# A fused attention and PReLU kernel on one core: the states of seven batches in one load, fills of 512 different columns written first, and a new order of all steps

## The chip, the core and the metric

The kernel runs on one core of one Trainium2 chip. TensorE (PE) multiplies matrices, VectorE (DVE), ScalarE (ACT) and GpSimd (POOL) work on elements, SyncE (SP) issues DMAs; DMAs are issued by ACT and POOL as well. Each engine takes its own instructions strictly in the order in which the program lists them, and waits on semaphores where it needs another engine's result. The metric is the device time of one execution in microseconds (us). Before the change it is 210.93 us, the median of 3 runs (210.7 to 211.01).

## The reference

```python
def _attn_ref(x, state):                      # x (8, 8, 512, 64), state (8, 8, 32, 64)
    scores = scale * np.matmul(x, state.transpose(0, 1, 3, 2))
    a = softmax(scores);  xread = np.matmul(a, state)          # tokens read the states
    scores2 = scale * np.matmul(state, x.transpose(0, 1, 3, 2))
    a2 = softmax(scores2); sread = np.matmul(a2, x)            # states read the tokens
    return np.concatenate([xread, sread], axis=2)

def _moe_ref(x, w_in, w_out, alpha):          # x (8 * 544, 512), d_ff = 2048
    h = x @ w_in
    g = np.maximum(h, 0.0) + alpha * np.minimum(h, 0.0)
    return g @ w_out
```

`softmax` stands here for the maximum, exponential, sum and division over the last axis that the reference writes out. Eight batches of 512 token rows and 32 state rows, 8 heads side by side in the 512 columns, go through attention and then through a two-layer network with a PReLU between.

## The kernel before

All work is cut into small steps, and one long string, ORDER (lines 18 to 96), lists them by name in the order in which they are written into the program. Nothing else sets the order of the work: an engine's queue is the list of those steps that fall to it. A step's letters `a`, `v` and `p` say that it goes to ACT, DVE or POOL. The last numbers of some steps name one of six single banks of PSUM (0 to 5) that the step's tile takes; the remaining two banks form one tile, tag `two`, that the scores `sc` of a batch and some of the `m` steps take in turn. A step that takes a bank waits until the readers of the bank's last tile have finished.

The steps that matter here, with b the batch:

- `stc`, `stt`, `sto`, `sbd`: cast, transposition on PE, copy out and pairing of the states that come early (lines 252 to 271). `lst` loads the other states on POOL's queue (line 194), `str` and `sro` transpose them and copy them out in two halves (lines 280 to 289). `lx`, `wi`, `wo` load x of a batch, a quarter of w_in, a quarter of w_out, all on POOL's queue (lines 156, 200, 206).
- Batch 0 has a path of its own: `cx` casts x, `xt` transposes it on PE, `xo` copies it out, `tsc` makes the scores, `smax`, `ssh`, `sexp`, `ssum`, `snorm` the softmax over the states, `at` and `ao` turn the result. `xt` and `xo` also serve batch 1.
- Other batches: `sc` makes the scores (line 314), `sb` turns them in blocks of 32 by 32 (DVE, line 352), `tm`, `nb`, `te` are the maximum, shift and exponential over the tokens (DVE, ACT, ACT, lines 430 to 455), `smax`, `ssh`, `sexp`, `ssum`, `snorm`, `wb` the softmax over the states. `sb`, `tm` and both `te` of a batch read the same tile `sc`. `tt` and `xd` are transpositions by DMA, `rd`, `rdo`, `rt`, `rto` the reads of the states.
- `m.b.f` multiplies the states of a batch with quarter f of w_in (PE, line 535) and `mo` copies the result out as `m`. `F.b.jc` is the first layer: the softmax weights times `m` (PE, 2 matmuls of 512 columns; batch 8 stands for all the state rows). `N` is the negative part (ACT, line 624), `G` the prelu (DVE, line 629).
- The second layer is `S` and `O` for batch 0, and for the others seven half-size products in place of eight: `W` and `U` make sums of the weights and of g, `P` multiplies (PE, 4 matmuls of 256 columns), `K` keeps a partial result, `Q` adds and sends it out.
- `Z` is a fill: a matmul on made-up numbers whose result nobody reads (line 229). Six of them stand ahead of ORDER (line 239).

Of the kernel before, what the change touches and what calls it, by code (L numbers as in the profile page):

```python
# [42 lines left out]
N.2.6 G.2.4 P.1.7.1.1.1 U.1.3.0.p G.2.6 ssh.p.3 P.1.7.0.1 sexp.3 ssum.3.0 P.1.7.1.0 tsum.3 P.1.5.0.0 K.1.4.a P.1.7.0.0
m.3.0.3.4 m.4.3 mo.3.0.a.1 mo.3.0.a.0 rd.3.2 U.1.4.1.p P.1.3.1.1 P.1.3.0.1 P.1.3.1.0 P.1.3.0.0 snorm.v.3 P.2.1.0.0.4
rdo.3.1.a mo.4.3.a P.2.1.1.0 rdo.3.0.a m.4.0.3.0 Q.1.0.1.a m.7.1.2.5 sc.4 mo.7.1.a.0 Q.1.1.1 U.2.1.1.p U.2.2.1.p
P.1.4.0.1 wb.3 P.1.4.1.0 F.3.10.2 mo.4.0.a.0 mo.4.0.a.1 F.3.3.3 sb.4 U.2.1.0.p F.3.1.0 P.2.1.1.1 N.3.10 tm.4 N.3.3
G.3.3 P.1.4.1.1 N.3.1 G.3.1 P.1.4.0.0 Q.1.1.0 P.2.1.0.1 nb.4.a te.4.1 F.3.12.3 G.3.10 F.3.15.0 mo.7.1.a.1 N.3.12
te.4.0 tt.4 F.3.8.1 G.3.12 smax.4 K.2.1.a F.3.2.5 F.3.9.2 N.3.9 N.3.2 sc.0 tm.0 P.2.2.1.1.3 N.3.15 G.3.9 G.3.15
P.2.2.0.1 P.2.6.1.1 P.2.6.0.1 P.2.2.0.0 N.3.8 G.3.8 U.2.2.0.p G.3.2 nb.0.a te.0.1 U.2.3.1.p P.2.6.0.0 P.2.6.1.0 te.0.0
tt.0 P.2.2.1.0 Q.2.0.0 K.2.2.a F.3.11.2 N.3.11 G.3.11 tsum.0 lx.5 xd.5 tsum.4 F.3.7.0 N.3.7 G.3.7 F.3.5.1 N.3.5 G.3.5  # L50
F.3.13.5 N.3.13 U.2.4.1.p G.3.13 ssh.p.4 F.3.6.3 P.2.5.0.0 P.2.5.1.0 P.2.7.1.1.2 N.3.6 F.3.14.0 G.3.6 sexp.4 U.2.3.0.p
N.3.14 G.3.14 F.3.4.1 P.2.7.1.0 P.2.5.0.1 P.2.7.0.1 N.3.4 U.2.4.0.p P.2.5.1.1 K.2.4.a ssum.4.5 rd.0.3 rdo.0.0.a
rdo.0.1.a rd.4.0 lx.6 G.3.4 P.2.7.0.0 Q.2.1.1 P.2.3.1.0 rt.0.3 rto.0.a snorm.v.4 rdo.4.1.a rdo.4.0.a xd.6 lx.7
U.3.1.1.p F.3.0.1 N.3.0 G.3.0 P.2.3.0.1 U.3.1.0.p P.2.4.0.1 P.2.3.1.1 P.2.3.0.0 Q.2.0.1.a m.4.1.3.0 mo.4.1.a.1
m.4.2.5.1 mo.4.2.a.1 sc.5 P.3.1.0.1.4 wb.4 mo.4.1.a.0 tm.5 mo.4.2.a.0 P.3.1.0.0 sb.5 F.4.2.0 N.4.2 G.4.2 F.4.1.1 N.4.1
xd.7 P.2.4.1.0 nb.5.a P.2.4.1.1 U.3.2.1.p P.2.4.0.0 Q.2.1.0 F.4.12.3 G.4.1 F.4.15.5 N.4.12 smax.5 N.4.15 G.4.15
F.4.3.0 N.4.3 F.4.10.2 N.4.10 P.3.2.1.0.1 G.4.3 P.3.2.0.0 te.5.0 G.4.12 P.3.2.1.1 P.3.1.1.0 te.5.1 P.3.1.1.1 P.3.2.0.1
G.4.10 K.3.1.a F.4.6.5 N.4.6 Q.3.0.0 F.4.9.0 F.4.4.3 F.4.13.2 N.4.9 G.4.6 G.4.9 N.4.4 G.4.4 U.3.2.0.p F.4.0.1
P.3.6.1.1 U.3.4.1.p P.3.6.1.0 N.4.13 G.4.13 P.3.6.0.0 N.4.0 G.4.0 P.3.6.0.1 K.3.2.a m.5.0.5.0 sc.6 mo.5.0.a.1
mo.5.0.a.0 tm.6 F.4.11.3 N.4.11 U.3.4.0.p F.4.7.2 N.4.7 sb.6 G.4.7 tt.5 F.4.8.1 F.4.14.0 N.4.14 N.4.8 nb.6.a G.4.8  # L60
te.6.0 G.4.11 smax.6 F.4.5.5 N.4.5 P.3.5.1.0 G.4.14 P.3.5.0.1 U.3.3.1.p P.3.5.0.0 U.3.3.0.p P.3.7.0.0.2 P.3.7.0.1
P.3.5.1.1 ssh.p.5 K.3.4.a P.3.7.1.0 te.6.1 P.3.7.1.1 P.3.3.1.1 sexp.5 G.4.5 rd.5.1 U.4.1.0.p U.4.2.0.p tsum.5
rdo.5.0.a sc.7 rdo.5.1.a m.5.3.3.0 mo.5.3.a.0 Q.3.1.1 ssum.5.5 tt.6 ssh.p.6 tm.7 P.3.3.0.0 mo.5.3.a.1 P.3.3.0.1
P.3.3.1.0 P.3.4.1.1 Q.3.0.1.a U.4.1.1.p U.4.2.1.p P.3.4.0.1 snorm.v.5 U.4.4.0.p m.6.1.1.3 mo.6.1.a.1 m.7.2.0.4
mo.7.2.a.1 P.3.4.0.0 P.3.4.1.0 Q.3.1.0 P.4.1.0.0.3 mo.7.2.a.0 P.4.1.0.1 P.4.1.1.0 P.4.2.1.0.4 wb.5 P.4.2.0.0 P.4.1.1.1
mo.6.1.a.0 U.4.3.1.p nb.7.a sexp.6 ssum.6.0 te.7.0 te.7.1 K.4.1.a sb.7 P.4.2.1.1 P.4.2.0.1 F.5.15.5 N.5.15 Q.4.0.0
F.5.7.1 N.5.7 F.5.13.2 N.5.13 P.4.6.1.1 P.4.6.0.0 G.5.13 G.5.15 G.5.7 P.4.6.1.0 P.4.6.0.1 F.5.6.4 F.5.9.2 F.5.1.5
snorm.v.6 K.4.2.a P.4.5.1.0 P.4.5.0.1 N.5.9 N.5.6 P.4.5.0.0 G.5.6 P.4.5.1.1 N.5.1 G.5.1 G.5.9 F.5.4.1 F.5.10.0 tsum.7
K.4.4.a N.5.4 F.5.12.4 N.5.12 U.4.4.1.p F.5.3.5 P.4.3.0.1 N.5.3 P.4.3.1.1 P.4.3.1.0 G.5.4 rd.6.2 G.5.12 G.5.3 tt.7
rd.7.1 tsum.6 m.7.3.4.5 m.6.0 N.5.10 G.5.10 rdo.6.0.a rdo.7.0.a mo.7.3.v.0 rdo.7.1.a rdo.6.1.a mo.7.3.a.1 rt.1.1  # L70
m.7.0.2.0 m.6.2.5.4 rto.1.v mo.7.0.a.1 P.4.3.0.0 F.5.8.1 mo.6.2.a.0 smax.7 Q.4.0.1.a U.4.3.0.p F.5.0.0 mo.6.2.a.1
F.5.2.5 wb.6 F.8.7.3 P.4.7.1.1.4 P.4.7.0.0 N.5.8 N.5.2 P.4.7.1.0 G.5.8 F.5.11.1 mo.7.0.a.0 N.8.7 G.5.2 G.8.7 F.8.4.2
F.8.8.5 N.5.0 G.5.0 N.5.11 N.8.4 F.5.5.3 G.5.11 N.8.8 G.8.8 N.5.5 G.8.4 F.8.6.0 N.8.6 F.5.14.1 ssh.p.7 F.6.4.5
P.5.2.1.0.2 N.5.14 G.5.5 U.5.1.0.p U.5.2.0.p P.4.7.0.1 P.5.1.1.1.3 G.5.14 P.5.2.1.1 U.5.1.1.p P.5.2.0.0 P.5.1.0.0
G.8.6 N.6.4 Q.4.1.1 P.4.4.1.0 G.6.4 P.4.4.1.1 P.4.4.0.0 sexp.7 P.4.4.0.1 P.5.1.1.0 ssum.7.1 snorm.v.7 P.5.1.0.1
Q.4.1.0 K.5.1.a P.5.2.0.1 Q.5.0.0 F.8.2.0 N.8.2 G.8.2 wb.7 F.6.6.5 N.6.6 G.6.6 F.6.13.1 N.6.13 F.6.11.4 F.6.15.2
N.6.15 G.6.15 N.6.11 G.6.11 F.8.15.0 N.8.15 P.5.6.1.0 U.5.2.1.p P.5.6.0.1 P.5.6.0.0 P.5.6.1.1 K.5.2.a F.7.4.5 G.6.13
# [739 lines left out]
```

## Time and profile before

| what | value |
|---|---|
| median of 3 runs | 210.93 us |
| the profiled execution | 211.77 us |
| its span, first to last instruction | 209.9 us |
| mean granted clock | 1.000 |
| PE, DVE, ACT, POOL busy | 95%, 87%, 70%, 75% |
| HBM read, written | 18.36 MB, 8.91 MB |

Rows of the timeline have the start in us, the duration, the engine, the line, the operation, the tiles (out<-in), the number of instructions merged, and in brackets the engine's idle time before them and what ended it. PEld is PE's loading of weights. Rows of the stages have the stretch, its length, then the busy time of PE, PEld, DVE, ACT and POOL with the number of instructions, the granted clock, the share of the DMA engines and GB/s. Rows of the chain have the start, the time spent, and the engine, tile and line it was spent on. A matmul's duration in a row includes its passage through the array, so that a run of matmuls is counted by the distance from start to start.

### The profile page before, as it was taken

What the parts mean: (1) busy time and instruction counts of PE and PEld (TensorE: products, weight loads), DVE (VectorE), ACT (ScalarE), POOL (GpSimd) and SP (SyncE); (2) the same over time, 40 slices, a digit from 0 to 9 for tenths busy, and PEclk for the clock granted to TensorE, in tenths of its full rate; (3) what the DMA queues carried; (4) which work ended last, traced back from release to release, by engine and by line L of the source; (5) the groups of instructions that cost most, each with busy time, mean ns of one, the idle gap of its engine ahead of it and who ended that gap; (6) DMA issues with size and microseconds to landing.
All of it is one profiled execution on the core that took longest, in us unless ns stands there. A gap on an engine that the chain in (4) does not pass through costs nothing.

```text
span 209.9 us, 5050 instructions
## 1 busy us (share of the span) xinstructions
PE 200.3 (95%) x2000; PEld 133.2 (63%) x2000; DVE 181.8 (87%) x269; ACT 146.6 (70%) x299; POOL 157.9 (75%) x96
## 2 busy tenths in 40 slices
...
GB/s 163 233 204 176 194 199 181 104 118 140 168 172 249 80 100 74 156 178 119 196 282 60 98 107 100 3 52 55 100 0 50 53 50 50 3 0 62 141 125 126
DMA packets 46215, 24.77 MB, mean 118 GB/s; under 512 B 24560, under 2 KB 45680, under 8 KB 46192
## 3 DMA queue, kind: packets, MB, share of 16 engines
...
q10 hardware_dynamic: 544, 0.13, 0.3%
...
HBM read 18.36 MB, written 8.91 MB: 130 GB/s over the span
## 4 chain that ended last, share of the span: by engine, by line
PE 78%; DVE 10%; ACT 7%; DMA 2%; issue 1%; ACTq 0%; DVEq 0%
PE px L732 24%; PE h L574 22%; PE pv L732 13%; PE py L732 6%; DVE g L630 5%; PE o L644 4%; PE h L583 3%; PE m_ps L525 2%; DMA x<-in_x_dram 2%; ACT neg L627 2%; ACT m L549 1%; PE sc L322 1%; ACT osb L661 1%; ACT e L449 1%; ACT XS L488 1%
## 5 line engine op out<-in xcount | busy, mean ns | idle before, releaser
L630 DVE SCALAR_TENSOR_TENSOR g<-neg,oma_sb,h 128x512 f16<-128x512 f32 (+1 forms) x144 | 94.8, 711 | 5.0 <-ACT neg L627 4.0
L627 ACT ACTIVATE neg<-h 128x512 f32<-128x512 f32 (+1 forms) x144 | 75.4, 594 | 12.6 <-PE h L574 10.1
L574 PE MATMUL h<-aT,m 128*128 128x512 f16 x256 | 64.2, 379 | 0.6 <-ACT osb L661 0.3
L732 PEld LDWEIGHTS <-gsum 128*128 128x128 f16 x480 | 46.6, 98 | 9.7 <-issue 0.7
L574 PEld LDWEIGHTS <-m 128*128 128x128 f16 x256 | 24.3, 98 | 24.7 <-issue 2.9
L732 PEld LDWEIGHTS <-g 128*128 128x128 f16 x360 | 34.8, 98 | 7.5 <-issue 1.7
L711 POOL TENSOR_TENSOR gsum<-gsum,g 128x1024 f16<-128x1024 f16 (+1 forms) x14 | 28.8, 2058 | 8.5 <-DVE gsum L711 7.7
L711 POOL TENSOR_TENSOR gsum<-g,gsum 128x1024 f16<-128x1024 f16 (+1 forms) x15 | 29.9, 1997 | 5.1 <-DVE gsum L711 3.2
L732 PE MATMUL px<-ws,gsum 128*128 128x256 f16 x240 | 31.1, 273 | 0.0
L711 POOL TENSOR_TENSOR gsum<-g 128x1024 f16<-128x1024 f16 (+1 forms) x14 | 28.7, 2057 | 3.1 <-DVE gsum L711 3.1
L711 POOL TENSOR_TENSOR gsum<-g,g 128x1024 f16<-128x1024 f16 (+1 forms) x12 | 24.5, 2049 | 6.9 <-DVE g L630 4.3
L748 ACT COPY kept<-px 128x512 f32<-128x512 f32 (+1 forms) x21 | 12.2, 580 | 23.1 <-PE px L732 22.9
L551 ACT CAST m<-m_ps 128x512 f16<-128x512 f32 x36 | 20.0, 626 | 1.5 <-PE m_ps L525 1.5
L392 POOL TENSOR_TENSOR ts<-ts,mx 128x1024 f32<-128x1024 f32 x7 | 13.4, 1913 | 6.7 <-ACT oq L763 4.1
L765 DVE TENSOR_TENSOR oq<-pv,kept 128x512 f32<-128x512 f32 (+1 forms) x16 | 10.4, 651 | 7.9 <-issue 4.4
L732 PE MATMUL py<-w_out_sb,g 128*128 128x256 f16 x120 | 16.6, 273 | 0.2 <-ACT osb L661 0.2
L644 PE MATMUL o<-w_out_sb,g 128*128 128x512 f16 x64 | 16.5, 380 | 0.0
L732 PE MATMUL pv<-ws,gsum 128*128 128x256 f16 x120 | 16.2, 273 | 0.0
L732 PE MATMUL px<-w_out_sb,g 128*128 128x256 f16 x120 | 16.1, 273 | 0.0
L732 PE MATMUL px<-w_out_sb,gsum 128*128 128x256 f16 x120 | 15.9, 273 | 0.0
L732 PE MATMUL pv<-ws,g 128*128 128x256 f16 x120 | 15.2, 273 | 0.0
L525 PE MATMUL m_ps<-w_in_sb,stT 64*32 64x512 f16 x256 | 12.3, 390 | 1.4 <-ACT e L449 1.1
...
## 6 DMA issues: line engine op xcount, KB each, us to landing
...
xg<-in_x_dram POOLq DMA_DIRECT2D x8, 512.0 KB, 6.9
w_in_sb<-in_moe_w_in_dram POOLq DMA_DIRECT2D x4, 512.0 KB, 9.0
w_out_sb<-in_moe_w_out_dram POOLq DMA_DIRECT2D x4, 512.0 KB, 10.7
x<-in_x_dram SPq DMA_DIRECT2D x2, 512.0 KB, 5.5
...
st<-in_state_dram POOLq DMA_DIRECT2D x1, 192.0 KB, 7.6
```

What stands on the lines that cost most here:

```text
L392: engine(e).tensor_tensor(blocks(cols(live["ts", b], j, S)), blocks(scored(b, j)), over_blocks(cols(live["mx", b], j, S // N)), ALU.subtract,)
L525: nc.tensor.matmul(t[N * k : N * (k + 1), :], st_head(b, h)[64 * r : 64 * r + 64, :], w_in_sb[64 * r : 64 * r + 64, c, 512 * f : 512 * (f ...
L551: copier(e)(m_tile(b, f)[:, g, :], t[g])
L574: nc.tensor.matmul(h.rearrange("p (r j s) -> p r j s", r=2, j=2), ms[b, f][:, g, 128 * j : 128 * (j + 1)], weights(b, g), start=(g == 0), ...
L583: nc.tensor.matmul(h, w_in_sb[:, c, 128 * jc : 128 * (jc + 1)], XS[:, c].rearrange("p q n b -> p (q n b)"), start=(c == 0), stop=(c == n_c ...
L627: nc.scalar.activation(neg, h, RELU, bias=0.0, scale=-1.0)
L630: nc.vector.scalar_tensor_tensor(g_tile(b, jc), negs.pop((b, jc)), oma_sb[:, jc : jc + 1], hs.pop((b, jc)), ALU.mult, ALU.add,)
L644: nc.tensor.matmul(outs[b, q], g_tile(b, jc)[:, 128 * q : 128 * (q + 1)], w_out_sb[:, jc, :], start=not begun and jc == 2 * jc2, stop=left ...
L711: engine(e).tensor_tensor(t, x(), y(), op)
L732: nc.tensor.matmul(pbanks[b, name][:, i, :], of(b, c)[:, j, 128 * i : 128 * (i + 1)], moving[:, 4 * c + j, :], start=not begun and j == 0, ...
L748: copier(e)(t, pbanks[b, "x"])
L765: nc.vector.tensor_tensor(osb, pbanks[b, name], kept[b, add], ALU.add)
```

## The change

Only batch 0's states are loaded ahead on ACT's queue; those of the seven other batches come in one load of 14 rows a partition on POOL's queue (192 KB written before, 224 KB now). Batch 1's own cast, transposition and copy go, and each half of `str` and `sro` has 7 groups of 128 columns in place of 6. The fills' operand is one tile of 512 different columns in place of 256 columns that were read twice, and it is written ahead of the first quarter of w_in on POOL's queue. ORDER is replaced as a whole: it has the same steps but for batch 1's three, at other places, in other banks, and some on other engines (three `U` go from POOL to DVE; of the copies of the start both `sro` go to ACT, all four `xo` of batch 1 to DVE, one `snorm` of batch 0 from POOL to DVE).

```diff
 ORDER = """
-stc.0.a Z.1.1 cx.1.0.v stt.0.2 cx.0.0.v sbd.1.v sto.0.v xt.0.1.0.3 lst xt.0.0.0.4 Z.5.1 xo.0.0.0.v sbd.0.a xo.0.1.0.a
-cx.0.1.a tsc.1.0.0 tsc.0.0 cx.1.1.v xt.0.1.1.1 xt.0.0.1.2 smax.0.0 Z.5.1 Z.3.1 xo.0.1.1.a tsc.1.1.4 xo.0.0.1.v tsc.0.1
-stc.1.a stt.1.5 sto.1.a ssh.v.0.0 m.0.0.1.3 sexp.0.0 Z.2.1 smax.0.1 ssh.v.0.1 m.1.0 wi.1 wi.2 mo.0.0.a.1 ssum.0.0
-sexp.0.1 lx.1 snorm.p.0.0 mo.1.0.a ssum.0.1 Z.0.1 Z.5.1 str.0.2 sro.0.a str.1.4 sro.1.v at.0.3 mo.0.0.a.0 ao.0.v
-m.0.1.0.5 mo.0.1.v.1 m.2.0.2.4 mo.0.1.a.0 snorm.p.0.1 at.1.1 ao.1.v oma mo.2.0.a.1 m.1.1 F.0.5.3 mo.1.1.v mo.2.0.a.0
-F.0.1.0 N.0.5 G.0.5 N.0.1 F.0.6.5 N.0.6 G.0.1 F.0.4.4 N.0.4 G.0.4 Z.1.1 G.0.6 F.0.0.2 N.0.0 wi.3 G.0.0 m.0.2 mo.0.2.a
...
-F.1.9.5 N.1.9 W.2.1.p W.4.1.p sc.2 tm.2 F.1.0.4 W.3.1.p G.1.9 N.1.0 G.1.0 sb.2 smax.2 F.1.13.2 N.1.13 nb.2.a te.2.1
-S.0.3.4.0 te.2.0 tsum.2 S.0.1.4 ssh.p.2 S.0.3.6 S.0.1.6 tt.2 xd.3 O.0.1.a F.1.6.5 N.1.6 G.1.13 S.0.0.7 F.1.2.4 N.1.2
...
-F.1.3.4 xd.4 wb.2 N.1.3 G.1.3 P.1.1.0.1.5 P.1.1.1.1 m.2.2.3.2 O.0.3.a sc.3 mo.2.2.a.0 mo.2.2.a.1 F.2.2.0 N.2.2
-F.2.12.3 N.2.12 U.1.2.1.p sb.3 F.2.0.4 N.2.0 P.1.1.1.0 tm.3 P.1.1.0.0 G.2.0 lx.0 G.2.12 P.1.2.1.0 K.1.1.a P.1.2.0.0
-Q.1.0.0 P.1.6.1.1 nb.3.a te.3.1 P.1.6.0.1 te.3.0 F.2.10.2 N.2.10 tt.3 smax.3 F.2.8.4 U.1.1.0.p U.1.2.0.p G.2.2
...
-Q.7.1.0 P.7.3.0.0 K.8.2.a P.8.5.0.1 U.8.4.1.p P.8.5.0.0 U.8.3.1.v U.8.4.0.p P.8.7.0.1.1 Q.8.0.0 P.8.7.0.0 K.8.4.v
-P.8.3.0.1 Q.7.0.1.v P.8.3.0.0 Q.8.1.1 P.8.4.0.0 Q.8.0.1.v P.8.4.0.1 Z.0.1 Q.8.1.0 Z.5.1
+stc.0.a lst Z.1.1 Z.2.1 stt.0.3 sbd.1.v wi.1 cx.1.0.v cx.0.0.a xt.0.0.0.4 xt.0.1.0.5 xo.0.0.0.v Z.0.1 lx.1 Z.1.1 Z.2.1
+sbd.0.v tsc.0.0.0 xo.0.1.0.a tsc.1.0 cx.0.1.a cx.1.1.v smax.0.0 xt.0.1.1.4 xt.0.0.1.1 xo.0.0.1.v xo.0.1.1.a tsc.1.1.5
+ssh.v.0.0 tsc.0.1 smax.0.1 ssh.v.0.1 sto.0.a sexp.0.0 ssum.0.0 m.0.0.2.4 wi.2 Z.1.1 Z.3.1 Z.0.1 mo.0.0.a.0 str.0.1
+mo.0.0.a.1 Z.3.1 str.1.2 snorm.p.0.0 at.0.0 sexp.0.1 ssum.0.1 wi.3 sro.0.a snorm.v.0.1 sro.1.a m.0.1.5.4 mo.0.1.v.0
+at.1.3 ao.0.a ao.1.v m.2.0.1.2 mo.2.0.v.0 m.1.0 mo.0.1.a.1 F.0.7.0 mo.1.0.a mo.2.0.v.1 F.0.1.5 N.0.7 oma G.0.7 wo.1
+N.0.1 G.0.1 F.0.6.3 N.0.6 F.0.0.4 G.0.6 m.1.1 xt.1.0.1.1 mo.1.1.a xt.1.1.0.2 xo.1.1.0.v xt.1.1.1.0 xo.1.1.1.v N.0.0
+F.0.4.5 N.0.4 F.0.5.3 xo.1.0.1.v m.0.2 F.0.2.2 wo.2 G.0.4 wo.0 F.0.3.0 lx.2 N.0.5 G.0.5 mo.0.2.a G.0.0 xt.1.0.0.1
...
+N.1.4 F.1.12.3 G.1.4 F.1.6.0 S.0.2.6 N.1.12 G.1.12 N.1.6 G.1.6 F.1.13.5 N.1.13 G.1.13 S.0.1.6 O.0.2.a F.1.5.3 N.1.5
+sc.2 tm.2 F.1.15.0 N.1.15 F.1.2.1 S.0.1.1 N.1.2 sb.2 G.1.2 nb.2.a S.0.1.7 O.0.1.a te.2.1 S.0.3.5.5 G.1.15 te.2.0 tt.2
+S.0.3.2 S.0.3.1 lx.3 xd.3 smax.2 W.2.1.p W.4.1.p W.3.1.p W.4.0.p F.1.0.4 N.1.0 G.1.5 S.0.3.0 F.1.9.1 G.1.0 S.0.0.7
+N.1.9 m.5.1 mo.5.1.a G.1.9 ssh.p.2 F.1.10.0 N.1.10 G.1.10 S.0.3.7 F.1.11.3 N.1.11 G.1.11 sexp.2 ssum.2.4 S.0.0.6
...
+P.1.1.1.1.3 P.1.1.0.1 sc.3 F.1.3.2 tm.3 F.2.9.4 N.1.3 G.1.3 N.2.9 F.2.12.1 N.2.12 F.2.3.5 nb.3.a te.3.0 P.1.2.1.0
+P.1.2.0.0 P.1.1.0.0 sb.3 G.2.12 P.1.1.1.0 te.3.1 tt.3 F.2.1.2 K.1.1.a G.2.9 Q.1.0.0 m.2.1 mo.2.1.a lx.4 smax.3
...
+te.5.1 F.3.3.3 N.3.3 F.3.1.4 N.3.1 wb.4 P.2.4.1.1 P.2.3.0.0 P.2.4.0.1 P.2.4.0.0 P.2.3.0.1 P.2.3.1.0 P.2.4.1.0 G.3.1
+m.7.2.1.0 mo.7.2.a.0 F.4.11.4 G.3.3 mo.7.2.a.1 sb.5 smax.5 P.2.3.1.1 Q.2.1.0 P.3.1.0.0.3 Q.2.0.1.a te.5.0 N.4.11
...
+U.3.3.1.p F.4.8.1 G.4.0 ssh.p.5 U.3.3.0.p N.4.8 F.4.5.2 N.4.5 G.4.5 nb.6.a G.4.8 P.3.5.1.0 P.3.5.0.0 K.3.4.a tsum.5
+te.6.1 sexp.5 xd.7 P.3.7.1.1.4 P.3.7.1.0 U.3.4.1.p P.3.3.0.1 P.3.7.0.1 P.3.7.0.0 U.3.4.0.p m.6.1.5.0 mo.6.1.a.1
+m.5.0.2.1 sb.6 Q.3.1.1 mo.5.0.a.1 mo.5.0.a.0 P.3.3.1.1 P.3.3.0.0 ssum.5.0 snorm.v.5 mo.6.1.a.0 P.3.3.1.0 P.3.2.1.1.1
...
+P.7.4.0.1 P.7.4.1.0 P.7.4.0.0 P.8.6.0.1 P.8.6.0.0 Q.6.0.1.v Q.7.1.0 Q.8.0.0 P.7.3.1.0 P.7.3.0.1 K.8.2.a P.8.5.0.0
+P.8.5.0.1 U.8.4.0.p K.8.4.a U.8.3.0.v P.8.7.0.0.0 P.8.7.0.1 U.8.4.1.v P.8.3.0.1 Q.7.0.1.v Q.8.1.1 P.8.3.0.0 P.8.4.0.1
+P.8.4.0.0 Q.8.0.1.a Z.3.1 Q.8.1.0
 """
...
-    n_j = (B * H * N - 2 * n0) // 128
-    st0_32 = [consts.tile([128, 2, D], F32, name=f"st0_32_{b}") for b in range(2)]
-    for b in range(2):
-        nc.scalar.dma_start(
-            st0_32[b], rows[n0 * b : n0 * (b + 1), :].rearrange("(g p) d -> p g d", p=128)
-        )
+    n_j = (B * H * N - n0) // 128
+    st0_32 = consts.tile([128, 2, D], F32)
+    nc.scalar.dma_start(st0_32, rows[:n0, :].rearrange("(g p) d -> p g d", p=128))
...
-        nc.gpsimd.dma_start(st, rows[2 * n0 :, :].rearrange("(p j) d -> p j d", j=n_j))
+        nc.gpsimd.dma_start(st, rows[n0:, :].rearrange("(p j) d -> p j d", j=n_j))
...
-    load_w_in(0)
-    pattern = consts.tile([128, 256], F16)
+    pattern = consts.tile([128, 512], F16)
     nc.gpsimd.iota(
-        pattern, pattern=[[37, 256]], base=-4800, channel_multiplier=29,
+        pattern, pattern=[[19, 512]], base=-4800, channel_multiplier=29,
         allow_small_or_imprecise_dtypes=True,
     )
+    load_w_in(0)
...
-        twice = pattern.unsqueeze(1).to_broadcast([128, 2, 256])
         for _ in range(n):
-            nc.tensor.matmul(
-                t.rearrange("p (a n) -> p a n", a=2), pattern[:, :128], twice, start=True, stop=True
-            )
+            nc.tensor.matmul(t, pattern[:, :128], pattern, start=True, stop=True)
```

128 lines of the change are left out of this document (60 added, 68 removed).

## The prediction

> **What bounds the kernel now.** I read the page's head first, then the busy times by stage, then the chain that ended last in order of time, and last the timeline where the chain leaves TensorE.
>
> ```profile
> PE 200.3 (95%) x2000; PEld 133.2 (63%) x2000; DVE 181.8 (87%) x269; ACT 146.6 (70%) x299; POOL 157.9 (75%) x96
> ```
>
> ```profile
> 25.00:41.00 16.00, 15.93 (x102) 6.63 (x98) 15.64 (x21) 13.17 (x26) 13.95 (x8) 1.00 1.09 166
> 41.00:57.00 16.00, 14.29 (x195) 6.77 (x194) 14.42 (x19) 13.57 (x30) 12.44 (x8) 1.00 0.83 140
> 57.00:100.00 43.00, 43.00 (x500) 29.01 (x500) 41.95 (x58) 38.16 (x80) 41.31 (x23) 1.00 0.84 142
> 100.00:150.00 50.00, 49.90 (x555) 35.89 (x553) 49.27 (x71) 39.32 (x86) 42.63 (x21) 1.00 0.43 100
> 150.00:205.00 55.00, 55.00 (x451) 44.03 (x450) 41.46 (x67) 25.01 (x51) 35.37 (x20) 1.00 0.17 60
> ```
>
> Columns are PE, PEld, DVE, ACT, POOL. From 57 us to 205 PE is never without work for more than 0.1 us, so only the time at which PE enters that stretch, or a new hole inside it, can change the end. Vector (DVE) is nearly as full: of 57 to 100 it has 43.00 - 41.95 = 1.05 us free. A stall of DVE there of more than about 1 us becomes a stall of PE.
>
> ```profile
> 17.82 6.01 DVE g L630 x9
> ...
> 56.97 1.51 PE h L574 x6
> ...
> 61.10 1.73 PE h L574 x8
> ...
> 205.28 0.89 PE pv L732 x8
> ```
>
> The chain runs through DVE's prelus (g, 6.01/9 = 0.67 us each) from 17.82, through ACT from 45.63, and from 56.97 through PE alone, where an F (two matmuls) costs 1.73/4 = 0.43 and a P group (four) 0.89/2 = 0.44. Why it passes to ACT at 45.63:
>
> ```profile
> 41.84 1.22 DVE L432 TENSOR_REDUCE nb<-sc 128x2 f32<-128x1024 f32 x1
> ...
> 42.98 1.40 DVE L630 SCALAR_TENSOR_TENSOR g<-neg,oma_sb,h 128x512 f16<-128x512 f32 x2
> 43.16 0.20 ACT L439 ACTIVATE nb<-nb 128x2 f32<-128x2 f32 x1
> ...
> 44.29 1.24 DVE L354 STREAM_TRANSPOSE ts<-sc 128x1024 f32<-128x1024 f32 x1
> ...
> 45.63 0.69 ACT L449 ACTIVATE e<-sc,nb 128x512 f16<-128x512 f32 x1 [2.26 <-DVE ts L354]
> ...
> 47.13 0.41 PE L525 MATMUL m_ps<-w_in_sb,stT 64*32 64x512 f16 x8 [1.09 <-ACT e L449]
> ```
>
> Batch 2's token exponentials (te, L449) have all that they compute with at 43.36, but start only when DVE has finished reading the same scores (sb, L354). Both only read `sc`. ACT idles 2.26 us, and PE then 1.09, because m.3.1 needs the two banks of `sc`.
>
> **The change, part by part.** The sum is made against the profiled execution: 211.77 us, of which 209.9 is its span; the median shown is 210.93, 0.84 below. A difference found in the span is taken over to the median as it is.
>
> *PE work.* Batch 1's own 4 transposes go and the rest grow from 2 x 12 to 2 x 14, beside batch 0's 4: 32 before, 32 after. Fills: 16 before, 16 after. F, P, S, m, rd, rt keep their numbers. So 0.
>
> *Start, fills and clock.*
>
> ```profile
> 1.25 0.91 POOL L201 DMA_DIRECT2D w_in_sb<-in_moe_w_in_dram  x1 [0.80 <-POOLq L801]
> ...
> 2.25 0.36 POOL L214 IOTA pattern<- 128x256 f16 x1
> ...
> 2.67 3.17 PE L234 MATMUL fill<-pattern 128*128 128x512 f16 x7 [2.67 <-POOL pattern L214]
> ...
> 5.66 0.94 DVE L175 CAST xg_first<-x 128x512 f16<-128x512 f32 x2 [4.48 <-DMA x<-in_x_dram]
> ...
> 7.16 0.63 PE L234 MATMUL fill<-pattern 128*128 128x512 f16 x1
> ...
> 8.24 0.61 PE L361 MATMUL tsc<-st_pairs,xT_first 128*128 128x64 f16 x8 [0.45 <-ACT xT_first L312]
> ...
> 11.82 0.45 PE L234 MATMUL fill<-pattern 128*128 128x512 f16 x1
> ...
> 12.55 0.61 PE L234 MATMUL fill<-pattern 128*128 128x512 f16 x2
> ```
>
> A fill takes (3.17 - 0.63)/6 = 0.42 us from the next in the first row and 0.61 - 0.45 or a little more, some 0.2, in the last, though the granted clock reads 1.00: PE runs at half its pace until about 11.8. The new iota stands ahead of the DMA, and has twice the columns: between 0.36 and 0.72 us, I take 0.6, the fixed part being small. It starts between 0.8 and 1.25 (POOL's first slot), so fills start at 1.4 to 1.9, not 2.67, and the eight ahead of the first transposes end at 4.8 to 5.3. That is no gain by itself: batch 0's x lands at 5.63 as before. Its two casts now run on DVE and ACT side by side, but the eight transposes begin when the slower ends, 6.3, as now. Behind them stand three fills instead of one: 2 x 0.42 = 0.85 us more, of which 0.45 falls into the gap that the 8.24 row shows. First scores at 8.6 instead of 8.24: +0.35. Two fills fewer stand in the next gap, which gives back nothing, as that gap waits for ACT and DVE copies. Writing the fills with other columns changes no duration (both stream 512).
>
> *Start, moved copies.*
>
> ```profile
> 10.08 0.68 DVE L392 TENSOR_TENSOR ts<-tsc,mx 128x512 f32<-128x512 f32 x1
> ...
> 14.07 0.83 ACT L287 COPY stT<-st_ps 128x768 f16<-128x768 f16 x1
> 14.21 0.90 DVE L287 COPY stT<-st_ps 128x768 f16<-128x768 f16 x1
> ...
> 15.41 0.69 DVE L551 CAST m<-m_ps 128x512 f16<-128x512 f32 x1
> ...
> 16.03 0.42 DVE L376 COPY aT<-at_ps 128x512 f16<-128x512 f16 x1
> ...
> 16.69 1.22 DVE L549 CAST m<-m_ps 128x1024 f16<-128x1024 f32 x1
> ...
> 16.92 2.55 ACT L627 ACTIVATE neg<-h 128x512 f32<-128x512 f32 x5
> ```
>
> Ahead of the first prelu DVE loses one x cast (0.47), one state copy (0.90), one aT copy (0.42), mo.1.1 (1.22) and a small state copy (0.3), and gains a second pairing copy (0.3), snorm (no DVE row; nearest the subtraction of the same shape, 0.68) and two half casts (1.38): 3.31 - 2.36, about 0.95 less. Two more copies of batch 1's xT (0.42 each) come behind it: net -0.1 us. ACT takes both state copies, now 896 wide: 2 x 0.83 x 896/768 = 1.94, against 0.83 and a small one. They stand between the second exponential and the last m casts: exponential 0.6, copies 1.9, ao 0.5, half cast 0.5, full cast 1.0, so that the first negative comes 4.5 us behind an exponential that starts about 12.6, as now. First negative 17.1 (overlap of neighbours taken off or not: 16.6 to 17.1), first prelu 17.2 to 17.7, against 17.82; with 0.84 of copies left over, DVE is 0.2 to 0.7 late. Bounds for the whole start: -0.4 (all chains hide but the arrivals of w_in) and +0.9 (scores +0.35 on top of the latest prelu). I take +0.4.
>
> *Queue of POOL's loads.* Now x of batch 1 goes ahead of w_in's third quarter (wi.2).
>
> ```profile
> 3.07 0.58 POOL L195 DMA_DIRECT2D st<-in_state_dram  x1
> ...
> 3.64 1.50 POOL L201 DMA_DIRECT2D w_in_sb<-in_moe_w_in_dram  x2
> ...
> 5.12 0.90 POOL L158 DMA_DIRECT2D xg<-in_x_dram  x1
> ...
> 13.08 0.86 PE L248 MATMUL st_ps<-ident,st 128*64 128x128 f16 x24
> ```
>
> ```profile
> st<-in_state_dram POOLq DMA_DIRECT2D x1, 192.0 KB, 7.6
> ...
> w_in_sb<-in_moe_w_in_dram POOLq DMA_DIRECT2D x1, 512.0 KB, 11.4
> xg<-in_x_dram POOLq DMA_DIRECT2D x1, 512.0 KB, 13.9
> ```
>
> The last column is the time from issue to landing. wi.2, issued at 3.64 + 0.75 = 4.4, landed near 15.8, and xg at 19.0, so one such load takes about 3 us of the queue and wi.1 landed near 13. Swapped, xg lands near 16.5, ahead of its use, and wi.2 near 19.1; its first user m.0.2 now stands behind F.0.5, which waits for the third prelu, about 19. Cost 0, if it lands before 20; every us later costs one. The one load of the states is 32 KB longer; it landed at 3.07 + 7.6 = 10.7, its transposes began at 13.08: hidden.
>
> *Batch 2's wait.* In the new order sb.2 follows tm.2 at once (the two prelus of the 42.98 row go behind), and ACT has N.1.15, N.1.2 and O.0.1 to do before te.2.1. sb.2 ends 1.22 + 1.24 = 2.5 us after the scores; ACT gets there at about 2.4. The idle 2.26 goes, and m.3.1 no longer follows the scores (m.5.1 does, later). Worth between 0 (DVE or PE late by as much anyway) and the PE time missing in that window, 16.00 - 14.29 = 1.7. I take -1.5, as ACT sets nearly all of those holes.
>
> *Batch 3's scores.* Here the order becomes tm.3, G.1.3, te.3.0, sb.3, te.3.1; before it was sb.3, tm.3 and then both te. If readers of the same banks go in listed order, as the 45.63 row shows, then, from the end of sc.3: DVE is free at 1.9 (1.22 + 0.67), but te.3.0 stands behind N.1.3, N.2.9 and N.2.12 (0.5 us each by the 16.92 row; the last one's matmuls end at 3 x 0.43 + 0.2 = 1.5) and nb (0.2), so it ends near 3.0; sb.3 ends 4.3; te.3.1 5.1. PE reaches m.2.1, which needs these banks, after 5 F and 4 P groups of 0.43 or 0.44: 3.9. It stalls 1.2 us, and DVE 1.1. Bounds 0 (te.3.0 and sb.3 free of each other) and +1.2; nearest row the 1.09 of m.3.1; I take +0.9, since DVE then enters a bit earlier than PE. [...]
>
> *Engines.* Three U steps go from POOL to DVE, all after 160 us, where DVE has 55.00 - 41.46 = 13.5 us free: 0.
>
> *End.*
>
> ```profile
> 205.12 1.04 PE L732 MATMUL pv<-ws,g 128*128 128x256 f16 x8
> ...
> 206.19 0.42 DVE L765 TENSOR_TENSOR oq<-pv,kept 128x256 f32<-128x256 f32 x1 [0.45 <-PE pv L732]
> ```
>
> The last P group, Q.8.1.0 and its DMA stay last, with the same number of P groups between each K and its bank's next product (two, 0.87 us, at the tightest): 0, bounds -0.1 and +0.3.
>
> **Sum**: +0.4 - 1.5 + 0.9 = -0.2 us: a profiled execution of 211.6, a median of **210.7**.
>
> **Rivals.**
>
> *The half pace ends early.* Between 2.67 and 11.8 PE was nearly always busy and stayed slow; it sped up after the stretch from 8.24, 3.6 us without a hole over 0.2. Now eight fills run from 1.4 to 4.8, 3.4 us without any. If that is enough, transposes, fills and scores take half: first scores near 7.5. Then w_in's second quarter (landing near 13, now a little later) holds m.0.1, and the first prelu comes near 16.7: the start is worth -0.5, the sum -1.1, **209.8**. For it: the 11.82 row. Against: 2.67 to 5.76 was as dense and did nothing. [...] Chance 0.22.
>
> *Slower: ACT and DVE wait for each other over the scores.* The interleaved listing te, sb, te also stands in batches 5 and 6. It decides when te starts later than sb's turn on DVE; in batch 6 only tsum stands between G.4.8 and sb.6, while te.6.1 waits behind K.3.4. DVE loses 1.1 in batch 3 and up to 1 in batch 6, against 1.05 us free: 1.2 + 1.0 in place of 0.9, **212.0**. For it: the 2.26 row and DVE's 41.95 of 43. Against: in batch 5 many steps lie between. Chance 0.30.
>
> *Batch 3's wait isn't there* (the exponential is done in time): -1.1, **209.8**. Chance 0.10; the 45.63 row speaks against it.
>
> **How the numbers follow.** Forecast 0.38 (own range 210.0 to 211.4), early clock 0.22, slower 0.30, no wait in batch 3 0.10. A measurement of this kernel tells about 0.2%, 0.42 us, from no change. Faster: 0.10 + 0.20 + 0.09 = 0.39; slower 0.10 + 0.29 = 0.39; within 0.22. The range leaves out the ends of the two outer cases: 209.2 to 212.3.
>
> **What would show it.** First fill near 1.5, first scores at 8.6 with a second fill 0.42 after the first (or near 7.5 with 0.2); first prelu 17.2 to 17.7; no idle over 0.5 before te.2.1; an idle of about 1 us before sb.3 and before m.2.1, ended by ACT e; PE without a hole after that. Wrong, if m.0.2 waits for w_in, if PE has holes of over 0.5 us after 65 us, or if the end lies more than 4.2 us behind the last P group.

## The result and the profile after

The change makes the kernel slower: 214.01 us (213.83 to 215.26, 4 runs) against 210.81 us (210.66 to 211.01, 4 runs), a ratio of 1.0159, 95% interval 1.0136 to 1.0182. The forecast of 210.7, its range and even its slower rival (212.0) lie below that.

The profiled execution took 213.87 us, its span 212.1. The page's head and the busy times by stage, in the same columns as before:

```profile
PE 200.1 (94%) x2000; PEld 131.5 (62%) x2000; DVE 182.9 (86%) x273; ACT 148.5 (70%) x297; POOL 153.6 (72%) x92
```

```profile
25.00:41.00 16.00, 15.83 (x110) 6.11 (x108) 15.79 (x21) 14.40 (x28) 13.68 (x8) 1.00 1.18 175
41.00:57.00 16.00, 16.00 (x199) 8.42 (x184) 15.03 (x20) 14.53 (x32) 14.38 (x9) 1.00 0.85 153
57.00:100.00 43.00, 40.69 (x488) 27.09 (x487) 40.59 (x56) 35.73 (x75) 37.62 (x21) 1.00 0.82 125
100.00:150.00 50.00, 48.45 (x545) 34.87 (x544) 47.36 (x68) 39.30 (x81) 41.94 (x22) 1.00 0.46 101
150.00:205.00 55.00, 55.00 (x444) 43.10 (x442) 43.12 (x73) 24.87 (x52) 33.30 (x17) 1.00 0.15 53
```

What the forecast wanted of 41 to 57 us happened: PE has no hole left (16.00, before 14.29). Behind it, where PE was never without work, it now lacks 43.00 - 40.69 = 2.3 and 50.00 - 48.45 = 1.6 us. DVE is less busy there as well (40.59 for 41.95, 47.36 for 49.27), so it isn't that DVE has more to do. The last stage is full as before.

The chain of waits, in order of time, says where. Its longest entries off PE behind 56 us, the one on PE that follows them, and the last one:

```profile
56.87 1.26 DVE ts L348
...
73.56 1.23 DVE nb L426
75.09 2.06 issue x2
77.15 1.45 ACT e L443 x4
...
119.59 1.00 DVE aT L414
120.67 1.19 DVE nb L426
121.85 1.12 DVE mx L381
123.41 1.06 ACT m L545 x2
125.10 1.45 ACT e L443 x4
127.55 1.91 PE px L726 x16
...
207.43 0.89 PE pv L726 x8
```

Before, the chain stayed on PE from 56.97 on, but for 3 us from 131.7, in a stretch (100 to 150) in which PE lacked 0.1 us in all. Now it leaves PE three times, with holes: in batch 3's scores, in batch 4's, and in batch 5's state reads. The end is as it was (last P group 4.7 us ahead of the end of the span, before 4.6).

**Batch 3**, timeline of the changed kernel:

```profile
56.06 0.69 ACT L443 ACTIVATE e<-sc,nb 128x512 f16<-128x512 f32 x1
...
56.87 1.25 DVE L348 STREAM_TRANSPOSE ts<-sc 128x1024 f32<-128x1024 f32 x1 [0.88 <-ACT e L443]
...
58.16 0.69 ACT L443 ACTIVATE e<-sc,nb 128x512 f16<-128x512 f32 x1 [1.32 <-DVE ts L348]
...
58.98 0.41 PE L519 MATMUL m_ps<-w_in_sb,stT 64*32 64x512 f16 x8 [1.24 <-ACT e L443]
```

te.3.0, sb.3, te.3.1, m.2.1: each waits for the one ahead of it. This is the wait that the forecast named. **Batch 4** has one that it did not name:

```profile
73.56 1.23 DVE L426 TENSOR_REDUCE nb<-sc 128x2 f32<-128x1024 f32 x1
...
74.70 1.24 DVE L414 STREAM_TRANSPOSE aT<-an 128x1024 f16<-128x1024 f16 x1
74.88 0.23 ACT L433 ACTIVATE nb<-nb 128x2 f32<-128x2 f32 x1
...
75.86 1.21 DVE L348 STREAM_TRANSPOSE ts<-sc 128x1024 f32<-128x1024 f32 x1
...
77.15 0.69 ACT L443 ACTIVATE e<-sc,nb 128x512 f16<-128x512 f32 x1 [2.04 <-issue]
...
79.12 0.40 PE L519 MATMUL m_ps<-w_in_sb,stT 64*32 64x512 f16 x4 [1.07 <-ACT m L545]
```

ACT has its shift at 75.1 and starts the exponential (te.4.1) at 77.15, when DVE has ended sb.4. Between tm.4 and sb.4 stands wb.3 (the row of 74.70), a block transposition of another batch. The profile names no releaser ("issue"), so that this is the cause is only a reading until a run changes the order of the two (a_sb4 below). **Batch 5**, one not named either:

```profile
121.78 1.20 DVE L381 TENSOR_REDUCE mx<-ts 128x32 f32<-128x1024 f32 x1
...
122.89 0.27 DVE L484 TENSOR_SCALAR XS<-sr_ps,r 128x64 f16<-128x64 f32 x1
...
123.20 0.31 ACT L482 ACTIVATE XS<-sr_ps,r 128x64 f16<-128x64 f32 x1 [2.41 <-DVE XS L484]
...
124.04 2.43 PE L568 MATMUL h<-aT,m 128*128 128x512 f16 x10 [0.46 <-ACT m L545]
...
127.55 1.69 PE L726 MATMUL px<-ws,gsum 128*128 128x256 f16 x14 [1.09 <-ACT kept L742]
```

The two halves of the state reads of batch 5 lie in one bank. The new ORDER gives one half to DVE (`rdo.5.0.v`, before `rdo.5.0.a`) and lists it behind smax.6; the other, on ACT, waits 2.41 us for it, and everything that ACT has behind it (mo.5.3, batch 7's exponentials, K.4.1) is late. The list of moved steps under "The change" lacks this one, and rdo.6.1 and rdo.7.1, which went from ACT to DVE too; there DVE waits 0.15 us for ACT's half, at 138, and PE meets no hole.

**Two starts.** One finding must stand ahead of all comparisons: the same program begins in one of two ways, early or late, by the time at which PE's pace doubles (0.42 us from one fill to the next, then 0.21). The same step of PE comes 1.0 us later in the one than in the other for the kernel before (its two profiles), and 1.6 us later for the changed kernel's order (the profiles of a_sb4 and a_m21 below against the changed kernel's). A second profile of the kernel before (b_again below, 210.85 us, span 208.9) shows it, its first rows on PE being:

```profile
2.67 3.06 PE L234 MATMUL fill<-pattern 128*128 128x512 f16 x7 [2.67 <-POOL pattern L214]
5.66 0.30 PE L248 MATMUL st_ps<-ident,st 128*64 128x128 f16 x4
...
8.82 0.59 PE L234 MATMUL fill<-pattern 128*128 128x512 f16 x2
```

The profile that the forecast was made from had the same seven fills from 2.67, but its four transposes took 0.42 instead of 0.30 and its two fills 1.06 instead of 0.59: PE ran at half pace until 11.8. That execution (211.77) was of the rarer kind. The changed kernel's profile has the early pace:

```profile
1.45 3.60 PE L230 MATMUL fill<-pattern 128*128 128x512 f16 x8 [1.45 <-POOL pattern L210]
...
6.63 0.81 PE L230 MATMUL fill<-pattern 128*128 128x512 f16 x3
7.27 0.48 PE L355 MATMUL tsc<-st_pairs,xT_first 128*128 128x64 f16 x8
```

So the profiles to compare are 213.87 and 210.85, 3.0 us apart, not 213.87 and 211.77.

**Where the 3.0 us arise.** Each PE step not yet begun at a time T, at its price from start to start in a dense stretch (F 0.43, P 0.44, and so on), added up and added to T, gives an estimate of the time at which PE would be done without another hole. Changed kernel minus kernel before, both with the early pace:

```
T (us)           25     41     57     65     85    122    130    190
difference    -0.13  +0.74  -1.66  -0.17  +1.21  +1.32  +3.30  +3.13
```

The start gives 0.1, the stretch of 25 to 41 takes 0.9, that of 41 to 57, with batch 2's wait in it, gives 2.4, batch 3 (57 to 65) takes 1.5, batch 4 (65 to 85) takes 1.4, batch 5 (122 to 130) takes 2.0. Other prices for the steps shift all columns alike, by 0.2 or so; the differences between columns hold to about 0.1.

### The profile page after: what moved, and what is told of

The parts are those of the page before. It is cut to its first block, busy times and chain, and to the rows that moved or that the text cites. A ratio compares the mean times of both kernels' runs of the same rounds, so it can differ in the third digit from the quotient of the medians.

```text
span 212.1 us, 5027 instructions
## 1 busy us (share of the span) xinstructions
PE 200.1 (94%) x2000; PEld 131.5 (62%) x2000; DVE 182.9 (86%) x273; ACT 148.5 (70%) x297; POOL 153.6 (72%) x92
## 4 chain that ended last, share of the span: by engine, by line
PE 74%; DVE 17%; ACT 4%; issue 2%; POOL 1%; POOLq 0%; DVEq 0%; ACTq 0%
PE px L726 23%; PE h L568 20%; PE pv L726 12%; DVE g L624 6%; PE py L726 5%; PE h L577 3%; PE o L638 3%; PE m_ps L519 3%; ACT e L443 2%; PE fill L230 2%; DVE mx L381 2%; DVE nb L426 2%; DVE aT L414 1%; DVE ts L348 1%; PE sr_ps L469 1%
## 5 line engine op out<-in xcount | busy, mean ns | idle before, releaser
L568 PE MATMUL h<-aT,m 128*128 128x512 f16 x256 | 65.4, 380 | 1.3 <-DVE g L624 0.5
L568 PEld LDWEIGHTS <-m 128*128 128x128 f16 x256 | 23.7, 97 | 26.1 <-issue 6.3
L726 PE MATMUL px<-ws,gsum 128*128 128x256 f16 x240 | 31.6, 273 | 1.1 <-ACT kept L742 1.1
L705 POOL TENSOR_TENSOR gsum<-g,g 128x1024 f16<-128x1024 f16 x12 | 25.5, 2123 | 8.9 <-DVE g L624 8.9
L705 POOL TENSOR_TENSOR gsum<-gsum,g 128x1024 f16<-128x1024 f16 x13 | 27.7, 2127 | 4.3 <-DVE gsum L705 3.4
L705 POOL TENSOR_TENSOR gsum<-g,gsum 128x1024 f16<-128x1024 f16 (+1 forms) x13 | 26.4, 2047 | 4.6 <-PE px L726 4.5
L545 ACT CAST m<-m_ps 128x512 f16<-128x512 f32 x35 | 19.3, 600 | 4.1 <-PE m_ps L519 4.1
L726 PE MATMUL py<-w_out_sb,g 128*128 128x256 f16 x120 | 16.0, 273 | 0.0
L726 PE MATMUL pv<-ws,gsum 128*128 128x256 f16 x120 | 15.1, 273 | 0.0
```

Source lines behind the costliest of these rows:

```text
L545: copier(e)(m_tile(b, f)[:, g, :], t[g])
L568: nc.tensor.matmul(h.rearrange("p (r j s) -> p r j s", r=2, j=2), ms[b, f][:, g, 128 * j : 128 * (j + 1)], weights(b, g), start=(g == 0), ...
L705: engine(e).tensor_tensor(t, x(), y(), op)
L726: nc.tensor.matmul(pbanks[b, name][:, i, :], of(b, c)[:, j, 128 * i : 128 * (i + 1)], moving[:, 4 * c + j, :], start=not begun and j == 0, ...
```

## The experiments

| kernel | median, range (us), runs | ratio to the kernel before, 95% interval |
|---|---|---|
| changed, sb.3 moved (a_sb3) | 213.59, 213.29 to 213.85, 4 | 1.0112, 1.0084 to 1.0139 |
| changed, sb.4 moved (a_sb4) | 214.16, 213.10 to 214.36, 4 | 1.0129, 1.0094 to 1.0164 |
| changed, rdo.5.0 on ACT (a_rdo5) | 212.29, 211.85 to 213.48, 10 | 1.0075, 1.0053 to 1.0097 |
| changed, all three (a_all3) | 210.58, 210.28 to 211.95, 10 | 0.998, 0.996 to 1.0 |
| before, sb.2 moved (b_sb2) | 209.82, 209.63 to 210.49, 5 | 0.9955, 0.994 to 0.997 |
| before, fills first, three more (b_fill) | 210.74, 210.44 to 210.76, 10 | 0.999, 0.9981 to 1.0 |
| all three, two early fills fewer (a_gap) | 211.76, 211.32 to 212.00, 4 | 1.0038, 1.0023 to 1.0053 |
| all three, PE steps moved (a_best) | 211.24, 211.08 to 212.56, 10 | 1.0023, 1.0009 to 1.0037 |
| before, unchanged (b_again) | 210.85, 1 | |
| two edits, m.2.1 later (a_m21) | 213.18, 211.82 to 213.23, 7 | 1.0075, 1.0045 to 1.0105 |
| two edits, rdo.5.0 earlier on DVE (a_rdov) | 211.40, 210.95 to 212.98, 10 | 1.0039, 1.0011 to 1.0066 |
| before, sb.2 and the rest (b_best) | 209.33, 209.13 to 209.34, 4 | 0.9917, 0.989 to 0.9945 |

The kernel before was run beside them, with medians of 210.86 to 210.90.

### The three waits, one by one and together

The theory: three waits between readers of one bank, at 1.0 to 1.9 us each, less what the start and batch 2 give. The rival: DVE is too full, and a wait that is mended turns up elsewhere.

```diff
-sc.3 F.1.3.2 tm.3 F.2.9.4 N.1.3 G.1.3
+sc.3 F.1.3.2 tm.3 sb.3 F.2.9.4 N.1.3 G.1.3
...
-P.1.2.0.0 P.1.1.0.0 sb.3 G.2.12
+P.1.2.0.0 P.1.1.0.0 G.2.12
```

> The changed kernel with sb.3 moved directly behind tm.3, so that DVE reads batch 3's scores before both exponentials. Theory (PE's holes come from readers of one bank on ACT and DVE that go in listed order): DVE's idle 0.88 ahead of sb.3 goes, te.3.1 starts near 57.2 instead of 58.16, m.2.1 near 58.0 instead of 58.98; time 1.0 us shorter, about 213.0. Rival (DVE is simply too full between 50 and 130 us, and the wait only shows it): G.1.3 comes 1.2 us later, what is gained before m.2.1 is lost again by batch 4's hole, and the time stays within 0.3 of 214.0.

213.59, or 0.4 less: nearer the rival, if a little outside its 0.3. PE's rows show why:

```profile
57.36 0.72 PE L726 MATMUL px<-w_out_sb,g 128*128 128x256 f16 x5 [0.41 <-DVE g L624]
...
58.45 0.41 PE L519 MATMUL m_ps<-w_in_sb,stT 64*32 64x512 f16 x8
...
61.78 1.05 PE L726 MATMUL px<-ws,gsum 128*128 128x256 f16 x8 [0.20 <-POOL gsum L705]
```

m.2.1 no longer waits and starts 0.53 us earlier. But the prelu G.1.3, now behind sb.3, holds a P step, and a sum of POOL that needs it holds another: the hole of 1.40 from start to start becomes 0.58 + 0.37 = 0.95. Counted by the same step of PE in both profiles, the gain is 0.36 us: from 14 to 56 us each step comes 0.2 later than in the changed kernel, from 65 us on each comes 0.17 earlier.

```diff
-mo.4.0.a.1 wb.3 F.2.10.3 N.2.10
+mo.4.0.a.1 sb.4 wb.3 F.2.10.3 N.2.10
...
-P.1.4.1.0 sb.4 nb.4.a
+P.1.4.1.0 nb.4.a
```

> The changed kernel with sb.4 moved ahead of wb.3 on DVE. Theory: sb.4 starts at 74.8 instead of 75.86 and te.4.1 at 76.0 instead of 77.15; the 1.2 us hole ahead of m.3.0's second half and sc.0 closes; time 1.2 us shorter, about 212.8. Rival (DVE too full): wb.3 is 1.2 us later, the first F of batch 3 waits for it instead, and the time stays within 0.3 of 214.0.

By its median (214.16) this would be no gain at all. But its profiled execution (214.36) had the late pace, with the scores at 8.51 instead of 7.27, and each step of PE from 10 us up to m.3.0 comes 1.6 us later than in the changed kernel's profile. From sc.0 on each comes 0.48 later: 1.13 us are made up there, PE's rows have no hole between m.3.0 and sc.0, and ACT's wait ahead of te.4.1 is 0.91 instead of 2.04. The effect is nearly the theory's 1.2; the median doesn't show it, since by their times three of the four began late.

```diff
-rd.5.4 rdo.5.0.v rdo.5.1.a
+rd.5.4 rdo.5.0.a rdo.5.1.a
```

> The changed kernel with both read-outs of batch 5's state reads on ACT (rdo.5.0 moved from DVE). Theory: ACT no longer waits 2.41 us for a DVE step that stands behind smax.6; mo.5.3 comes 1.5 to 2 us earlier, the holes ahead of F.5.4 (0.62) and P.4.6 (1.25) close; time 1.5 to 1.9 us shorter, 212.1 to 212.5. Rival (ACT or DVE is behind by itself at that point): a hole of at least 1 us remains ahead of P.4.6 or the next step; time at least 213.4.

212.29, 1.7 less, with both holes gone; in the profile (211.85, span 210.1) the span is 2.0 shorter, all of it between 123 and 130 us. As the theory said.

> The changed kernel with all three edits together. Theory: the three effects add to 3.5 to 4.1 us, time 209.9 to 210.5, so at or a little under the kernel before (210.8): what the start and batch 2 gained shows at the end. Rival (DVE too full): PE meets a later hole, ended by DVE, between 65 and 130 us, and the time is 212 or more.

210.58, 3.4 less than the changed kernel (0.1 above the theory's range), and the spans differ by 212.1 - 208.6 = 3.5. Counted by the same step of PE it is 0.36 in batch 3, 1.13 in batch 4 and 1.98 in batch 5, as in the three kernels alone: the effects add up. In batches 4 and 5 DVE is not too full for that; in batch 3 some 1.1 of the 1.5 us of the table above remain, mostly in the two holes that a_sb3 showed:

```profile
57.00:100.00 43.00, 42.68 (x504) 28.71 (x505) 41.04 (x57) 37.39 (x81) 39.87 (x21) 1.00 0.82 127
100.00:150.00 50.00, 50.00 (x556) 35.91 (x555) 48.84 (x71) 40.31 (x84) 43.94 (x23) 1.00 0.45 109
```

So the loss lies in three places of the order. The load of the states and the fills have no part in it that the medians show. By their times, though, some 16 of 49 runs of the changed kernel and its variants with the same fills began late, against 4 or 5 of 55 of the kernel before.

### Is it PE's wait or DVE's, the position or the shared bank?

In one kernel batch 3's interleaving stayed, with the edits of batches 4 and 5, and m.2.1, which needs the banks, was put later:

```diff
-m.2.1 mo.2.1.a lx.4 smax.3 F.2.15.1 U.1.2.1.p P.1.6.1.1 N.2.3 F.2.0.4 F.2.11.0
+lx.4 smax.3 F.2.15.1 U.1.2.1.p P.1.6.1.1 N.2.3 F.2.0.4 m.2.1 mo.2.1.a F.2.11.0
```

> The changed kernel with the edits of batches 4 and 5, and in batch 3 te.3.0, sb.3, te.3.1 left interleaved, but m.2.1, which needs their banks, moved behind F.2.15.1, P.1.6.1.1 and F.2.0.4 on PE, with its copy behind it. Theory (the hole of 1.40 is only PE's wait for those banks): other PE work covers it, and DVE's 0.88 of idle is made up, time 0.3 to 0.7 us less than with all three edits (210.6), 209.9 to 210.3. Rival (DVE's idle is what costs, since DVE is full there): PE waits 0.7 us or more for a prelu or a sum by 70 us, time 210.5 to 211.5.

```profile
58.49 1.25 DVE L348 STREAM_TRANSPOSE ts<-sc 128x1024 f32<-128x1024 f32 x1 [0.89 <-ACT e L443]
59.66 1.37 DVE L624 SCALAR_TENSOR_TENSOR g<-neg,oma_sb,h 128x512 f16<-128x512 f32 x2
```

```profile
60.42 0.59 PE L568 MATMUL h<-aT,m 128*128 128x512 f16 x2 [1.06 <-DVE g L624]
...
63.58 0.41 PE L519 MATMUL m_ps<-w_in_sb,stT 64*32 64x512 f16 x8 [0.60 <-ACT m L543]
```

The theory was wrong: nothing is gained. By their times four of the seven runs began late, and so did the profile, so that its rows stand 1.6 us later than the changed kernel's; but the lowest run is 211.82, still 1.2 above a_all3's median and above the rival's range. In the mechanism the rival was right: with m.2.1 out of the way PE runs into F.2.15.1 and waits 1.06 us for a prelu that stands on DVE behind sb.3, and 0.89 of that is the time in which DVE stood still. The edit has a cost of its own beside it, the 0.60 us of the last row, in which PE waits for ACT's late copy of m.2.1. Counted by the same step of PE, the kernel loses 0.8 us more in batch 3 than the changed kernel does, so that DVE's idle time is part of the price, but not shown to be all of it.

In another, rdo.5.0 stayed on DVE, but ahead of smax.6, with the edits of batches 3 and 4:

```diff
-tm.7 mo.7.1.a.0 smax.6 rd.5.4 rdo.5.0.v rdo.5.1.a
+tm.7 mo.7.1.a.0 rd.5.4 rdo.5.0.v smax.6 rdo.5.1.a
```

> The changed kernel with the edits of batches 3 and 4, and rdo.5.0 left on DVE but moved ahead of smax.6, so that the bank's two readers stay on two engines and only the position changes. Theory (the cost is the place in DVE's queue): ACT's wait for it falls from 2.41 to about 1.2, the two holes of batch 5 (1.87) fall to 0.3 to 0.9, time 210.9 to 211.5. Rival (two engines on one bank cost by themselves): the holes stay, 212.2 or more. Other rival (ACT has 1.2 us to spare): no hole, 210.6.

```profile
120.82 0.31 ACT L482 ACTIVATE XS<-sr_ps,r 128x64 f16<-128x64 f32 x1 [1.29 <-DVE XS L484]
```

211.40, with a hole of 0.86 left ahead of P.4.6, as the theory said. Counted by the same step of PE, the place in DVE's queue is worth 1.12 of batch 5's 1.98 us. The other 0.86 is still there with the two halves on two engines, as ACT waits 1.29 us for DVE's half. In batches 6 and 7, where the first reader ran at once, two engines on one bank cost next to nothing (0.15 us of DVE's time); in batch 5 the cost followed how long the first reader had to wait in its own queue (ACT's wait for it was 2.41 us, and 1.29 with rdo.5.0 ahead of smax.6).

### Batch 2's wait, on the kernel before

```diff
-sc.2 tm.2 F.1.0.4 W.3.1.p G.1.9 N.1.0 G.1.0 sb.2 smax.2
+sc.2 tm.2 sb.2 F.1.0.4 W.3.1.p G.1.9 N.1.0 G.1.0 smax.2
```

> The kernel before with sb.2 moved directly behind tm.2, ahead of the two prelus G.1.9 and G.1.0. Theory (ACT's exponentials wait for DVE's reading of the same scores): te.2.1 starts near 44.3 instead of 45.63, PE's hole of 1.09 ahead of m.3.1 goes, time 1.0 to 1.3 us shorter, 209.6 to 209.9. Rival (the two prelus, 1.25 us later, hold the next P or F steps by as much): a hole of about 1 us elsewhere before 57 us, time within 0.4 of 210.9.

209.82, 1.04 less, though PE's rows show the rival too: ACT's wait ahead of te.2.1 falls from 2.26 to 0.94 us, PE's hole ahead of m.3.1 goes, and a smaller one comes.

```profile
43.93 0.60 PE L574 MATMUL h<-aT,m 128*128 128x512 f16 x2 [0.59 <-DVE g L630]
```

F.1.6.5 waits for its bank, that is for G.1.9, now behind sb.2 (0.75 from start to start).

### The start

On the kernel before, the pattern (256 columns, as there) written first, and three fills more:

```diff
-stc.0.a Z.1.1 cx.1.0.v stt.0.2
+stc.0.a Z.1.4 cx.1.0.v stt.0.2
...
-    load_w_in(0)
     pattern = consts.tile([128, 256], F16)
...
+    load_w_in(0)
```

> The kernel before with the fills' pattern written ahead of w_in's first quarter and three more fills ahead of the first transposes (10 in place of 7). Theory (PE's pace doubles some 5 us after PE became busy, if no hole of about 0.9 us interrupts it): transposes and scores before 11 us run at 0.2 instead of 0.42 us a step, first scores near 7.4 instead of 8.24, first prelu 0.5 to 1.0 us earlier than 17.82, time 0.5 to 0.9 us shorter, 210.0 to 210.4. Rival (copies on ACT and DVE and the landing of w_in set the first prelu): first prelu within 0.2 of 17.8, time within 0.4 of 210.9.

210.74: the fills start at 1.24, the first scores at 7.97, hardly earlier than the 8.07 of b_again, as they wait for ACT's copy of xT (PE idle for 0.97 us), and the first prelu at 16.72, for 16.84. The rival was right on the gain; its 17.8 for the first prelu is the late start's. All ten runs lie within 0.32 us, and none has the time of a late start. But the 20 runs of the kernel before beside them, 210.69 to 211.11, have none either (the late ones, up to 211.82, are among 19 runs beside a_sb3 and 16 beside b_best), so that the early fills prevent a late start is not shown.

On the changed kernel with all three edits, two fills fewer:

```diff
-stc.0.a lst Z.1.1 Z.2.1 stt.0.3
+stc.0.a lst stt.0.3
```

> The kernel with all three edits, without the two fills Z.1.1 and Z.2.1 ahead of the first transposes, so that PE pauses for about 0.9 us between 4.2 and 5.1. Theory (that pause decides when the pace doubles): the half pace lasts to about 10 us in every execution, first scores near 8.1 instead of 7.27, first prelu 1.2 to 1.6 us later, time 1.2 to 1.6 us longer than with all three edits alone (210.6), 211.8 to 212.2. Rival (the pace doubles at a fixed time, or with the amount of work done): first prelu within 0.3 of 16.8, time 210.4 to 210.8.

211.76, 1.2 longer than a_all3, its lowest run 0.7 above a_all3's median.

```profile
1.45 2.74 PE L230 MATMUL fill<-pattern 128*128 128x512 f16 x6 [1.45 <-POOL pattern L210]
5.49 0.42 PE L242 MATMUL st_ps<-ident,st 128*64 128x128 f16 x4 [1.30 <-ACT st L248]
...
7.17 1.49 PE L230 MATMUL fill<-pattern 128*128 128x512 f16 x3
```

After a pause of 1.30 us the fills at 7.17 still take 0.42 each, where the changed kernel's at 6.63 take 0.21. The first prelu comes at 18.38, 1.6 later than in a_all3. In this execution the six fills ahead of the pause did not by themselves bring the full pace. That the pause decides is not shown: a_sb4 and a_m21 have all eight fills, and their profiles began late too.

The kernel before once more, without an edit:

> The kernel before, unchanged, for a second profile. Theory (its executions have two starts, by the time at which PE's pace doubles, and the profile that the forecast was made from shows the rarer, later one): with a time near 210.9 the pace doubles near 6 us, the scores' steps take 0.2 instead of 0.42 us, first prelu near 16.9 instead of 17.82. Rival (the start is the same in all executions, the 0.84 us lie elsewhere): first prelu at 17.8 again.

Early pace, and the first prelu at 16.84: the theory. 16.84 is also when the changed kernel's first prelu starts.

### Two attempts at a better kernel

```diff
-stc.0.a lst Z.1.1 Z.2.1 stt.0.3
+stc.0.a lst Z.1.1 Z.2.2 stt.0.3
...
-P.1.1.1.0 te.3.1 tt.3 F.2.1.2
+F.2.1.2 P.1.1.1.0 te.3.1 tt.3
...
-P.1.6.0.0 P.1.6.1.0 G.2.3 K.1.2.a lx.0 F.2.13.1
+F.2.13.1 P.1.6.0.0 P.1.6.1.0 G.2.3 K.1.2.a lx.0
```

> The kernel with all three edits, with one fill more ahead of the first transposes (it covers a late landing of the states), and with two first-layer steps moved on PE: F.2.1.2 ahead of P.1.1.1.0 and F.2.13.1 ahead of P.1.6.0.0, which wait for DVE and POOL there (holes of 0.58 and 0.37). Theory: both holes close, 0.5 to 0.9 us shorter than with all three edits alone, and the executions spread less: 209.7 to 210.1. Rival (DVE is full): PE waits as long for DVE a little later, time 210.4 to 210.7.

A miss: 211.24, 0.7 more than a_all3, and one run of 212.56 still.

```profile
57.41 0.28 PE L726 MATMUL px<-w_out_sb,g 128*128 128x256 f16 x1 [0.41 <-DVE g L624]
...
61.92 0.59 PE L568 MATMUL h<-aT,m 128*128 128x512 f16 x2 [0.30 <-DVE g L624]
```

The first row has one matmul, the last of P.1.1.0.0: it is this step that waits for G.1.3, not P.1.1.1.0 behind it, and an F moved in between covers nothing. F.2.13.1, moved ahead, waits for a prelu itself. And the added fill moves the first transposes from 5.06 to 5.40, and all behind them by 0.3.

```diff
-tm.2 F.1.0.4 W.3.1.p G.1.9 N.1.0 G.1.0 sb.2
+tm.2 sb.2 F.1.0.4 W.3.1.p G.1.9 N.1.0 G.1.0
...
-F.1.6.5 N.1.6 G.1.13 S.0.0.7 F.1.2.4 N.1.2 S.0.3.2 m.3.1
+S.0.0.7 S.0.3.2 F.1.6.5 N.1.6 G.1.13 F.1.2.4 N.1.2 m.3.1
```

> The kernel before with sb.2 directly behind tm.2, S.0.0.7 and S.0.3.2 ahead of F.1.6.5 on PE (they cover the 0.75 that F.1.6.5 waited for G.1.9 with sb.2 moved alone), the pattern written first and three fills more. Theory: batch 2's wait goes without a new one, and every execution has the early pace: 208.9 to 209.3, with a spread under 0.5. Rival (DVE's 1.24 us ahead of the two prelus is paid later): 209.7 to 209.9, no better than sb.2 alone.

209.33, all four runs within 0.21 us: a ratio of 0.9917 (0.989 to 0.9945) to the kernel before, faster than both kernels. It is the kernel before with batch 2's wait taken out (1.4 less than b_fill's 210.74) and with the two edits of b_fill. Counted by the same step of PE against b_again, the start is worth 0.3 and the stretch of 41 to 57 us 1.3. By their times no run began late; with four runs that says little. PE's busy time of 41 to 57 us:

```profile
41.00:57.00 16.00, 15.55 (x192) 7.86 (x191) 15.44 (x20) 15.03 (x32) 13.80 (x8) 1.00 0.94 159
```

## Why the prediction was wrong

The steps in its own order:

- **The base.** "A difference found in the span is taken over to the median as it is": the 0.84 us between profile and median were not outside the span, they were the late pace of that one execution (b_again: 208.9 of span, 210.85 of time). The start was thus measured against a start that the median does not have.
- **Start +0.4.** Measured -0.1 against the kernel's usual start: the first prelu at 16.84 in both. The first fill came at 1.45 as forecast. The rival of the early pace was right about the pace (scores at 7.27) and wrong about the gain, because the kernel before usually has it too.
- **POOL's loads 0.** Right: m.0.2 ran at 19.47, in turn, without a wait for w_in.
- **25 to 41 us.** Not in the sum, and the difference there is +0.9. What makes it was not tried; about 0.4 of it are holes of 0.2 between first-layer steps from 35 to 38 us, in a stretch in which DVE is busy for 15.79 of 16.00.
- **Batch 2 -1.5.** The wait is gone: te.2.1 starts at 43.76 with less than 0.2 us of idle time on ACT before it. By the table the stretch of 41 to 57 gives 2.4; on the kernel before, the wait alone was worth 1.1 to 1.3 there (b_sb2 and b_best, by the same step of PE). The rest are three holes of 0.3 to 0.4 from 49 to 56 us that the new order lacks; two of them remain in b_best, so those two at least hang on something else, which was not tried. That this stretch and the one ahead of it come to -1.5 together, the forecast's figure, is chance.
- **Batch 3 +0.9.** The mechanism was right (te.3.0, then sb.3, then te.3.1, and m.2.1 behind), the size 1.5 by the table. The reason given for taking less than the strict 1.2, "since DVE then enters a bit earlier than PE", was wrong: DVE's own idle of 0.88 costs too, as a_m21 showed. But only 0.4 of the 1.5 went when sb.3 was moved; what the rest hangs on stays open. In these rows a reader on the other engine starts only when the one ahead of it has ended (waits of 0.88 and 1.32 us here, 2.41 in batch 5), and the strict 1.2 was nearer to the table's size.
- **All else 0.** This is the step that failed: the sum had no term for the readers of a bank in batches 4 and 5. They cost 1.4 and 2.0 us by the table, and 1.1 and 2.0 when mended: 3.1 of the 3.3 us between the forecast of 210.7 and the 214.01 measured. The batch 4 one was missed because only the listing te, sb, te was looked for; there sb stands ahead of both te, but wb.3 ahead of it. The batch 5 one was missed because the engines were compared only for U, where DVE has room, while `rdo.5.0` went from ACT to DVE with a partner left on ACT. The slower rival had the kind of loss right, a second wait over a bank's readers, and the place wrong. Batch 6, where it had put the second loss, shows none: sb.6 started at 114.29 without a wait of note.
- **End 0.** Right (4.7 against 4.6 us behind the start of the last P group).

With the terms as the table has them, -0.1 + 0.9 - 2.4 + 1.5 + 1.4 + 2.0 = +3.3, against 3.2 between the spans of 208.9 and 212.1. Of batches 3, 4 and 5, 4.9 us in the table, 3.5 are shown by mending them (a_all3: 0.4 + 1.1 + 2.0); of the 2.4, 1.1 to 1.3 by b_sb2 and b_best; the rest of batch 3, the rest of the 2.4 and the +0.9 stand only in the table.
